# Attention feeding a two-GEMM block on one core: two pairs of TensorE steps joined into one step each, from batch 2 on

## The chip, the cores and the metric

The kernel runs on one core of a Trainium2 chip, in one launch. The metric is the device time in microseconds (us) of an execution, as the median over runs. The core has five engines that run side by side and wait for each other by semaphores: TensorE (PE, matrix multiplies), VectorE (DVE), ScalarE (ACT), GpSimd (POOL) and SyncE (SP, which only issues DMAs here). Each runs its own instructions in the order in which the program holds them.

## What is computed

The inputs q, k and v have 8 batches, 8 heads, 576 positions and 64 features each. The attention part adds two results: a pooled attention, over means of four positions, whose rows are repeated four times, and a local one, in which a position sees those less than 4 away. The sum, laid out as 4608 tokens by 512 features, goes through two matrix products with h * cos(h) between them.

```
factor = 4; Sd = S // factor; scale = 1.0 / np.sqrt(D)
q_d, k_d, v_d = (a.reshape(B, H, Sd, factor, D).mean(axis=3) for a in (q, k, v))
out_up = np.repeat(sm_attn(q_d, k_d, v_d), factor, axis=2)
mask = np.abs(pos[:, None] - pos[None, :]) < factor
scores = np.where(mask, scale * np.matmul(q, k.transpose(0, 1, 3, 2)), -1e9)
out_local = np.matmul(softmax(scores), v)
x = (out_up + out_local).transpose(0, 2, 1, 3).reshape(B * S, H * D)
h = x @ w_in                      # 512 -> 2048
return (h * np.cos(h)) @ w_out    # 2048 -> 512
```

## The kernel before

**The attention** works by pairs of heads: 8 batches of 4 pairs, called p0 to p3 here. For a pair, `u_qk` loads q and k and sums each over groups of four positions (`qkd`), `u_v` loads v in two layouts and sums it likewise (`vd`, `vl`), and three functions compute:
- `u_s`: on PE the local scores (`l_mm`, line 518: 48 small fp32 matmuls, 32 by 32 outputs, from q and k) and the pooled scores (`d_mm`, line 526: 4 matmuls of 72 by 144 from `qkd`), into two PSUM banks. Then, mostly on DVE, the mask (line 537), the maxima (542 and 550), their subtraction (389), the exponent on ACT, the sums (577), the reciprocal (581) and the scaling (583) of `sml` (local) and `smd` (pooled).
- `u_t`: the transposes of `smd` on PE (line 609, two steps, one a head) with copies into `ptd`, and of `sml` on DVE (600) into `ptl`.
- `u_pv`: on PE the pooled values (`d_mm`, line 626: 4 matmuls from `vd` and `ptd`) and the local values (`l_mm`, line 637: 48 matmuls from `vl` and `ptl`), the sum of both on DVE (645), and the split of the sum into a high and a low fp32r part, `xh` (660) and `xl` (389).

**The GEMMs** go over 12 token tiles of 384. `x` lies in a ring of four buffers, so the names x0 to x3 stand for tiles 0 to 3, then 4 to 7, and so on. For a tile and a chunk of 128 of the 2048 hidden features, `gemm1` (line 688) makes 12 matmuls of 128 by 384; ACT and DVE compute h * cos(h) from them (lines 697 to 706, `tr`, then `gh` and `gl`); `gemm2` (line 724) makes 9 matmuls of 128 by 512 with the results of two chunks earlier, in three steps. The first three tiles take four chunks in turn each, the rest run through all 16. The weights (`wi`, `wo`) come from 64-bit numbers; `w_split` takes them apart on ACT, DVE and POOL (lines 410 to 423) into a high and a low part, the low one by a subtraction (389).

**The order** is not written by hand. Each function hands its pieces of work to a planner, as `pl.op(engine, duration, function, reads, writes)`. The planner knows which piece depends on which, runs a list scheduling with estimated durations forth and back several times, keeps the best, and lets some pieces choose between two engines. The program is then emitted in the order of planned starts, so that one piece (a step) is never parted: all its instructions stand together on their engine, ahead of all later ones. The GEMM steps keep their order among themselves (`pe_order`); the attention steps fall in between. Where PE is planned to idle in the first 300 us, filler matmuls of an identity (line 841) are put in. `NEARLY = 2` separates the first two batches, which are computed before the GEMMs can run at full rate, from the others. The PSUM banks of the attention (`pa`) are three in rotation.

An example of a step as it is handed over:

```
pl.op("PE", 0.95, l_mm, r=[q, k], pw=banks, w=loc)
pl.op("PE", 0.65, d_mm, r=[qkd], pw=banks, w=poo)
```

Of the kernel before, what the change touches and what calls it, by code (L numbers as in the profile page):

```python
# [48 lines left out]
NEARLY = 2  # L49
# [241 lines left out]
def _dve(n):  # L291
    return n * 0.001042 + 0.065
# [7 lines left out]
def attn_ffn_kernel(ctx: ExitStack, tc: tile.TileContext, qT, kT, vdn, vl, w_in, w_out, out):  # L300
# [8 lines left out]
    pl = Plan()  # L309
# [92 lines left out]
    def w_split(k, c):  # L402
# [27 lines left out]
                k=([P, SP_], 1, 1, 0), ptd=([HD, 2, 2, SD], 1, 1, 0),  # L430
# [16 lines left out]
    def bank(b, kind):  # L447

        if b == 0:
            tags = ("pa.0", "po.0", "pa.1", "po.1") if kind == "s" else ("ph.0", "ph.1", "pa.2")  # L450
            return psum(tags[int(pl.turn("early" + str(kind == "s"), len(tags))[-1])])
        return psum(pl.turn("pa", 3))
# [47 lines left out]
    def u_s(b, pr):  # L500
        pl.name = "u_s"
        u = st[(b, pr)]
        q, k, qkd = u["q"], u["k"], u["qkd"]
        sml, smd = ub(b, pr, "sml"), ub(b, pr, "smd")
        banks = [bank(b, "s") for _ in range(2)]
        loc, poo = [pl.buf(None) for _ in banks], [pl.buf(None) for _ in banks]
# [5 lines left out]
        def l_mm():  # L512

            for n in range(2 * NSEG):
                for h in range(2):
                    for e in range(2):
                        hs, o, c = slice(64 * h, 64 * h + 64), (8 * (n // 4) + 4 * e + n % 4) * BQ, LQ + BS * (n % NSEG)
                        pe.matmul(banks[n // NSEG].get()[64 * h + BS * e:64 * h + BS * (e + 1), c:c + BS],  # L518
                                  q.get()[hs, o:o + BS], k.get()[hs, o:o + BS], start=True, stop=True)
        pl.op("PE", 0.95, l_mm, r=[q, k], pw=banks, w=loc)  # L520

        def d_mm():
            for i in range(2):
                for h in range(2):
                    hs = slice(64 * h, 64 * h + 64)
                    pe.matmul(banks[h].get()[:HD, i * SD:(i + 1) * SD], qkd.get()[hs, 0, i * HD:(i + 1) * HD], qkd.get()[hs, 1, :],  # L526
                              start=True, stop=True)
        pl.op("PE", 0.65, d_mm, r=[qkd], pw=banks, w=poo)


        mxl, su = sb("mxl", 2, [P, 2 * NSEG]), sb("su", 2, [P, 2 * NSEG + 4])
# [16 lines left out]
        for h in range(2):  # L548
# [3 lines left out]
            if not early:  # L552
                using(banks[h], pl.op("DVE", _dve(2 * SD), lambda h=h: dve.tensor_tensor(
                    out=smd.get()[:, h], in0=dq(h), in1=mxd.get()[:, h].unsqueeze(2).broadcast_to([HD, 2, SD]), op=ALU.subtract),
                    r=[poo[h], mx], pw=[smd]))
# [59 lines left out]
    def u_pv(b, pr):  # L615
        pl.name = "u_pv"
        u = st.pop((b, pr))
        ptl, ptd, vd, vt = (u[n] for n in ("ptl", "ptd", "vd", "vl"))
        xd, xs = ub(b, pr, "xd"), ub(b, pr, "xs")
        banks = [bank(b, "v") for _ in range(2)]  # L620
        poo, loc = pl.buf(None), [pl.buf(None) for _ in banks]

        def d_mm():
            for kh in range(2):
                for h in range(2):
                    pe.matmul(banks[0].get()[64 * h:64 * h + 64, 2 * SD:3 * SD], vd.get()[:, kh, 64 * h:64 * h + 64],  # L626
                              ptd.get()[:, h, kh, :], start=(kh == 0), stop=(kh == 1))
        pl.op("PE", 0.64, d_mm, r=[vd, ptd], pw=[banks[0]], w=[poo])

        def l_mm():  # L630
            for a in range(NSEG // 2):
                for i in range(4):
                    for e in range(2):
                        for h in range(2):
                            r = slice(64 * h + 32 * e, 64 * h + 32 * e + 32)
                            o = (4 * a + i) * BQ
                            pe.matmul(banks[e].get()[64 * h:64 * h + 64, o:o + BQ], vt.get()[r, a, i, :], ptl.get()[r, 4 * a + i, :BQ],  # L637
                                      start=True, stop=True)
        pl.op("PE", 1.52, l_mm, r=[vt, ptl], pw=banks, w=loc)

        evac(SD, xd.get, lambda: banks[0].get()[:, 2 * SD:3 * SD], banks[0], xd, scale=0.25)
        xd.w[-1].deps += poo.w
# [8 lines left out]
        while lo < S:  # L651
# [9 lines left out]
                  r=[xs], w=[done], pw=[x_b[tt]], alts=[("DVE", _dve(m / 2), lambda hi=hi, src=src: dve.tensor_copy(hi(), src()))])  # L661
            sub(m, lambda tt=tt, a=a, m=m: x_tile(tt)[1][:, pr, a:a + m], src, lambda hi=hi: hi().bitcast(F32),
                r=[xs, done], pw=[x_b[tt]])
# [94 lines left out]
    def unit(t, step, ahead, *a):  # L758
        for d, f in ((-ahead, u_qk), (0.01 - ahead, u_v), (0.0, u_s), (step, u_t), (2 * step, u_pv)):
            at(t + d, f, *a)  # L760

    for i in range(NPAIR):
        for t, f in ((-10.0 + 0.5 * i, u_qk), (-8.4 + 0.5 * i, u_v), (-7.5 + i, u_s), (-6.5 + i, u_t), (-5.5 + i, u_pv)):
            at(t, f, 0, i)
# [15 lines left out]
    for i in range(NPAIR):  # L780
        for t, f in ((-4.0 + 0.5 * i, u_qk), (-2.4 + 0.5 * i, u_v), (-0.9 + i, u_s), (-0.1 + i, u_t), (0.7 + i, u_pv)):
            at(t, f, 1, i)
# [96 lines left out]
```

## Time and profile before

| | |
|---|---|
| median of 3 runs | 1031.43 us (1028.47 to 1034.59) |
| the profiled execution | 1031.63 us, of it 1029.5 us from the first to the last instruction |
| mean granted PE clock | 0.983 |
| matmuls of an attention pair on PE | 96 each in local scores and local values (each fp32 matmul shows twice), 8 each in the other three steps |

The profile is of one execution. A page gives busy times, the span in 40 slices and the costliest groups; other views give the single instructions in order of time (start, duration, engine, line, output<-input, shape), in brackets the idle time of the engine before an instruction and the one that ended it, or busy times by stretches of the span. Durations of matmuls overlap, so that the distance between two starts tells what one costs.

### The profile page before, as it was taken

To read this page: it belongs to the slowest core of one execution; us is meant where nothing else is said; L and a number is where in the kernel's file an instruction comes from. 1 tells how busy PE (TensorE), PEld (TensorE's weight loads), DVE (VectorE), ACT (ScalarE), POOL (GpSimd) and SP (SyncE) were. 2 spreads that over 40 slices of the span, in tenths; PEclk is the share of its full clock that TensorE was granted. 3 is DMA by queue.
4 is the path that set the end of the run, shared out by engine and by line. 5 is a ranking of instruction groups with operands and counts; after the bars stand their busy time and mean duration, and the time that the engine had idled before them with its cause. 6 is when DMAs were issued, how large, how long until landed. Compare 5 with 4: busy or idle time off the path is not lost.

```text
span 1029.5 us, 25935 instructions
## 1 busy us (share of the span) xinstructions
PE 1003.0 (97%) x11068; PEld 864.9 (84%) x11068; DVE 676.9 (66%) x1353; ACT 610.6 (59%) x1176; POOL 228.8 (22%) x274
## 2 busy tenths in 40 slices
PE   7889999999999999999999999999999999999998
PEld 4557788889988888889898888888888888899997
DVE  6699889996478668564738856755646865543443
ACT  2546577786566666565646655655655765655554
POOL 5596424433135201010103300101002410000000
PEclk8988899999999999999999999999999999999999
DMA  9762751434245312100202401200101310000000
GB/s 265 237 221 85 242 183 46 61 59 62 32 106 144 76 50 75 59 25 28 76 6 76 133 28 38 96 25 28 55 27 43 120 51 1 32 1 1 31 1 31
DMA packets 36450, 76.11 MB, mean 74 GB/s; under 512 B 3440, under 2 KB 11632, under 8 KB 36336
## 3 DMA queue, kind: packets, MB, share of 16 engines
q1 hardware_dynamic: 32448, 67.38, 20.6%
q0 software_dynamic: 3888, 7.08, 5.0%
q8 instruction: 87, 1.43, 0.6%
q14 instruction: 27, 0.22, 0.1%
HBM read 57.93 MB, written 16.52 MB: 72 GB/s over the span
## 4 chain that ended last, share of the span: by engine, by line
PE 81%; DVE 10%; DMA 4%; ACT 2%; issue 2%; POOL 0%; SPq 0%; ACTq 0%; DVEq 0%; POOLq 0%
PE bank L688 35%; PE bank L724 35%; PE bank L637 3%; PE bank L518 3%; PE bank L526 2%; DMA q<-qT 2%; PE bank L609 2%; DMA wdi<-w_in 1%; PE bank L626 1%; DVE su L577 1%; DVE qkd L480 1%; DVE mxd L550 1%; PE bank L841 1%; DVE gl L389 1%; DVE tr L700 1%
## 5 line engine op out<-in xcount | busy, mean ns | idle before, releaser
L724 PE MATMUL bank<-wo,gh 128*128 128x512 f32 x1152 | 363.3, 396 | 0.0
L724 PEld LDWEIGHTS bank<-wo,gh 128*128 128x128 f32 x1152 | 210.0, 188 | 35.8 <-issue 2.3
L724 PE MATMUL bank<-wo,gl 128*128 128x512 f32 x576 | 228.0, 396 | 0.6 <-POOL su L535 0.6
L699 ACT ACTIVATE tr<-bank,bmagic 128x384 f32<-128x384 f32 x192 | 111.0, 579 | 134.0 <-PE bank L688 122.5
L703 DVE SCALAR_TENSOR_TENSOR tr<-tr,bank 128x384 f32<-128x384 f32 x192 | 105.3, 549 | 121.7 <-ACT tr L698 121.4
L700 DVE SCALAR_TENSOR_TENSOR tr<-tr,bank 128x384 f32<-128x384 f32 x192 | 105.5, 550 | 97.5 <-ACT tr L699 97.3
L697 ACT ACTIVATE tr<-tr 128x384 f32<-128x384 f32 x192 | 100.7, 524 | 84.4 <-DVE tr L700 83.7
L705 ACT ACTIVATE gh<-tr 128x384 fp32r<-128x384 f32 x177 | 92.5, 523 | 90.7 <-DVE tr L703 89.0
L389 DVE TENSOR_TENSOR gl<-tr,gh 128x384 fp32r<-128x384 f32 x160 | 97.3, 609 | 68.6 <-ACT gh L705 67.2
L724 PEld LDWEIGHTS bank<-wo,gl 128*128 128x128 f32 x576 | 108.0, 187 | 24.8 <-POOL su L535 1.0
L688 PE MATMUL bank<-x0h,wi 128*128 128x384 f32 x384 | 109.9, 347 | 0.7 <-DVE tr L703 0.7
L688 PE MATMUL bank<-x1h,wi 128*128 128x384 f32 x384 | 107.6, 341 | 0.0
L688 PE MATMUL bank<-x2h,wi 128*128 128x384 f32 x384 | 107.1, 339 | 0.0
L688 PE MATMUL bank<-x3h,wi 128*128 128x384 f32 x384 | 106.9, 339 | 0.0
L389 POOL TENSOR_TENSOR gl<-tr,gh 128x384 fp32r<-128x384 f32 x32 | 38.1, 1189 | 301.3 <-DVE gh L706 215.8
L698 ACT ACTIVATE tr<-tr 128x384 f32<-128x384 f32 x192 | 100.8, 525 | 6.1
L688 PEld LDWEIGHTS bank<-x0h,wi 128*128 128x128 f32 x384 | 72.1, 193 | 3.7 <-DVE tr L703 0.8
L688 PEld LDWEIGHTS bank<-x1h,wi 128*128 128x128 f32 x384 | 70.7, 189 | 2.9 <-issue 0.8
L688 PEld LDWEIGHTS bank<-x2h,wi 128*128 128x128 f32 x384 | 70.2, 188 | 2.8 <-DVE sml L537 0.6
L688 PEld LDWEIGHTS bank<-x3h,wi 128*128 128x128 f32 x384 | 70.2, 188 | 2.5 <-issue 0.6
L688 PE MATMUL bank<-x0l,wi 128*128 128x384 f32 x192 | 65.8, 342 | 0.0
L688 PE MATMUL bank<-x3l,wi 128*128 128x384 f32 x192 | 64.6, 336 | 0.5 <-POOL x3l L389 0.5
(192 smaller groups left out, 1473.0 us busy)
## 6 DMA issues: line engine op xcount, KB each, us to landing
vl<-vl SPq DMA_DIRECT2D x26, 384.0 KB
out<-ob SPq DMA_DIRECT2D x36, 256.0 KB
wdi<-w_in SPq DMA_DIRECT2D x16, 512.0 KB
wdo<-w_out SPq DMA_DIRECT2D x16, 512.0 KB
q<-qT SPq DMA_DIRECT2D x26, 292.0 KB
k<-kT SPq DMA_DIRECT2D x26, 292.0 KB
vd<-vdn SPq DMA_DIRECT2D x26, 288.0 KB
out<-ob POOLq DMA_DIRECT2D x27, 256.0 KB, 5.7
```

The lines of the kernel that those rows point to most:

```text
L389: f = lambda e: lambda: e.tensor_tensor(out=out(), in0=in0(), in1=in1(), op=ALU.subtract)
L518: pe.matmul(banks[n // NSEG].get()[64 * h + BS * e:64 * h + BS * (e + 1), c:c + BS], q.get()[hs, o:o + BS], k.get()[hs, o:o + BS], start=T ...
L526: pe.matmul(banks[h].get()[:HD, i * SD:(i + 1) * SD], qkd.get()[hs, 0, i * HD:(i + 1) * HD], qkd.get()[hs, 1, :], start=True, stop=True)
L637: pe.matmul(banks[e].get()[64 * h:64 * h + 64, o:o + BQ], vt.get()[r, a, i, :], ptl.get()[r, 4 * a + i, :BQ], start=True, stop=True)
L688: pe.matmul(ph.get()[:, :m], w[:, i, kc, :], x[:, kc, :], start=(n == 0), stop=(n == 3 * KC - 1))
L697: act.activation(tr.get(), tr.get(), AF.Sin, scale=PI)
L698: act.activation(tr.get(), tr.get(), AF.Square)
L699: pl.op("ACT", _act(m, True, 1), lambda: act.activation(tr.get(), h(), AF.Identity, bias=bmagic), r=[ph], w=[tr])
L700: pl.op("DVE", _dve(m), lambda: dve.scalar_tensor_tensor(out=tr.get(), in0=tr.get(), scalar=MAGIC, in1=h(), op0=ALU.subtract, op1=ALU.subt ...
L703: pl.op("DVE", _dve(m), lambda: dve.scalar_tensor_tensor(out=tr.get(), in0=tr.get(), scalar=0.5, in1=h(), op0=ALU.subtract, op1=ALU.mult), ...
L705: pl.op("ACT", _act(m, False), lambda: act.activation(gh.get(), tr.get(), AF.Copy), r=[tr], w=[gh], alts=[("DVE", _dve(m / 2), lambda: dve ...
L724: pe.matmul(o, (gh, gh, gl)[k].get()[:, sl], wo.get()[:, (0, 1, 0)[k]], start=(c == c0 and k == 0), stop=(c == c1 - 1 and k == 2))
```

## The change

For batches 2 to 7, `u_s` hands over its local and pooled scores as one step, local ones first, which reads q, k and `qkd`; `u_pv` hands over its pooled and local values as one step, pooled ones first, which reads `vd`, `ptd`, `vl` and `ptl`. The planned durations of the joined steps are 1.55 and 2.1, where the parts had 0.95 + 0.65 and 0.64 + 1.52. No matmul is added or removed, and batches 0 and 1 keep their separate steps. Since one plan is made for the whole program, the order and the choice of engines move in other places too.

```
-        pl.op("PE", 0.95, l_mm, r=[q, k], pw=banks, w=loc)
+        if b < NEARLY:
+            pl.op("PE", 0.95, l_mm, r=[q, k], pw=banks, w=loc)
...
-        pl.op("PE", 0.65, d_mm, r=[qkd], pw=banks, w=poo)
+        if b < NEARLY:
+            pl.op("PE", 0.65, d_mm, r=[qkd], pw=banks, w=poo)
+        else:
+            pl.op("PE", 1.55, lambda: (l_mm(), d_mm()), r=[q, k, qkd], pw=banks, w=loc + poo)
...
-        pl.op("PE", 0.64, d_mm, r=[vd, ptd], pw=[banks[0]], w=[poo])
+        if b < NEARLY:
+            pl.op("PE", 0.64, d_mm, r=[vd, ptd], pw=[banks[0]], w=[poo])
...
-        pl.op("PE", 1.52, l_mm, r=[vt, ptl], pw=banks, w=loc)
+        if b < NEARLY:
+            pl.op("PE", 1.52, l_mm, r=[vt, ptl], pw=banks, w=loc)
+        else:
+            pl.op("PE", 2.1, lambda: (d_mm(), l_mm()), r=[vd, ptd, vt, ptl], pw=banks, w=[poo] + loc)
```

After the change the lines named above stand 0 to 8 lines further down (526 is 527, 537 is 541, 609 is 613, 626 is 630, 637 is 642, 645 is 653, 688 is 696, 724 is 732, 841 is 849). Where the order is shown, the names stand for buffers with their numbers; in batches 0 and 1 a pair's tensors borrow the space of weights that come later, so that `wxi` and `wxo` are scores and values there too.

**In the full part**, on PE, about 640 us after the start, around chunks 14 and 15 of a tile. Before, one pair's scores and the values of the pair ahead of it stand in three places:

```order
L518 MATMUL bank<-k,q 32x32 x48
L526 MATMUL bank<-qkd 72x144 x4
L724 MATMUL bank<-wo_2977,gh 128x512 x2
L724 MATMUL bank<-wo_2977,gl 128x512
L626 MATMUL bank<-ptd,vd 64x144 x4
L688 MATMUL bank<-x2h,wi_3164 128x384
...
L637 MATMUL bank<-ptl,vl 64x24 x48
L724 MATMUL bank<-wo_3075,gh 128x512 x2
```

And at the same pairs with the change:

```order
L518 MATMUL bank<-k,q 32x32 x48
L527 MATMUL bank<-qkd 72x144 x4
L732 MATMUL bank<-wo_2848,gh 128x512 x2
L732 MATMUL bank<-wo_2848,gl 128x512
...
L630 MATMUL bank<-ptd,vd 64x144 x4
L642 MATMUL bank<-ptl,vl 64x24 x48
L696 MATMUL bank<-x2h,wi_3081 128x384
```

The pooled values moved behind the whole gemm2 and stand with the local ones; three islands of small matmuls became two. Counted over the program from the first gemm1 of tile 1 on, there are 80 such islands before and 74 now.

**In batch 1, between its pairs p2 and p3**, on PE. Before (`wxo_191` holds p2's pooled scores, `wxo_928` and `wxo_918` are p3's k and q, `wi_1378` is chunk 2 of w_in):

```order
L609 MATMUL bank<-ident,wxo_191 72x72 x4
L688 MATMUL bank<-x0h,wi_1378 128x384
L688 MATMUL bank<-x0l,wi_1378 128x384
...
L518 MATMUL bank<-wxo_928,wxo_918 32x32 x48
L526 MATMUL bank<-wxi_208 72x144 x4
L609 MATMUL bank<-ident,wxo_191 72x72 x4
```

With the change (chunk 2 is `wi_1358`, and p3's k and q are `wxo_925` and `wxo_910`; `wxi_270` with `wxo_315` are p1's local values, `wi_1477` is chunk 3):

```order
L696 MATMUL bank<-x0h,wi_1358 128x384
...
L642 MATMUL bank<-wxi_270,wxo_315 64x24 x48
L732 MATMUL bank<-wo_949,gh 128x512 x2
...
L613 MATMUL bank<-ident,wxo_191 72x72 x8
L518 MATMUL bank<-wxo_925,wxo_910 32x32 x48
L527 MATMUL bank<-wxi_208 72x144 x4
L630 MATMUL bank<-wxi_194 64x144 x4
L696 MATMUL bank<-x0h,wi_1477 128x384
```

The gemm1 of tile 0, chunk 2, which stood between p2's transposes and p3's scores, now stands ahead of p1's local values, and p3's scores follow p2's transposes directly.

**In batch 1, between p0 and p1**, on PE and DVE. Before, PE has p0's pooled and local values with nine fillers between them and no gemm1:

```order
L609 MATMUL bank<-ident,smd 72x72 x8
L518 MATMUL bank<-xxl 32x32 x48
L526 MATMUL bank<-wxi_126 72x144 x4
L626 MATMUL bank<-ptd,vd 64x144 x4
L841 MATMUL bank<-ident_b 128x512
...
L637 MATMUL bank<-ptl,vl 64x24 x48
```

With the change the gemm1 of tile 0, chunk 1 (`wi_1123`) stands there, behind four fillers:

```order
L613 MATMUL bank<-ident,smd 72x72 x8
L518 MATMUL bank<-xxl 32x32 x48
L527 MATMUL bank<-wxi_126 72x144 x4
L630 MATMUL bank<-ptd,vd 64x144 x4
...
L696 MATMUL bank<-x0h,wi_1123 128x384
L696 MATMUL bank<-x0l,wi_1123 128x384
...
L642 MATMUL bank<-ptl,vl 64x24 x48
```

The low half of that chunk's weight was made by POOL before; with the change DVE makes it, behind the subtraction of p1's maxima (`wxi_270` are p1's local scores):

```order
L541 TENSOR_TENSOR wxi_270<-bank,mask 128x192 x2
L554 TENSOR_REDUCE mxd<-bank 72x2
L546 TENSOR_REDUCE mxl<-wxi_270 128x12
L389 TENSOR_TENSOR wxi_270<-wxi_270,mxl 128x384
L389 TENSOR_TENSOR wi_1123<-xxh,wi_1123 128x512
L413 TENSOR_SCALAR xxh<-xxh 128x512
```

That gemm1, which stood behind p2's scores, now stands ahead of p0's local values, and so ahead of p1's transposes on PE. DVE has 178 instructions up to the last sum (line 645) of batch 1 before and 176 with the change; up to the second formula step (line 703) of the 25th gemm1 it has 348 and 334.

## The prediction, made before the result

> **What bounds the kernel now.** I read the head of the page first, then busy time by stretches, then who made TensorE (PE) wait after 150 us.
>
> ```profile
> span 1029.5 us, 25935 instructions
> PE 1003.0 (97%) x11068; PEld 864.9 (84%) x11068; DVE 676.9 (66%) x1353; ACT 610.6 (59%) x1176; POOL 228.8 (22%) x274
> ...
> PEclk8988899999999999999999999999999999999999
> ```
> ```profile
> 53.00:115.00 62.00, 53.64 (x989) 37.48 (x985) 56.68 (x110) 32.82 (x90) 44.43 (x47) 0.82 0.53 174
> ...
> 114.15:1025.50 911.35, 907.64 (x9059) 803.37 (x9054) 586.09 (x1172) 557.00 (x1018) 155.59 (x173) 1.00 0.21 57
> ```
> ```profile
> PE bank L609 <- DVE smd L583: 1.4, 5, 0.4
> PE bank L688 <- DVE tr L703: 0.7, 1, 0.7
> PE bank L688 <- POOL x3l L389: 0.5, 1, 0.5
> ```
>
> The columns of the stretches are length, then busy PE, weight loads, DVE, ACT, POOL, then the clock and the DMA. From 114.15 us to the last matmul PE is busy 907.64 of 911.35 us at clock 1.00; after 150 us it waits 2.6 us in all (1.4 + 0.7 + 0.5). In that part the time is the sum of PE's work, so only less PE work, or a new wait, can move the end. Ahead of it stands a part where PE is not the bound: from 53 to 115 us DVE is busy 56.68 of 62 us while PE runs at clock 0.82, partly on filler matmuls. This is the attention of batch 1's four pairs (p0 to p3), which gemm1 of token tile 1 has to have. So there are two places: what an attention step costs PE in the full part, and when the full part begins.
>
> **Term 1: fewer interruptions of the GEMM stream.** No matmul is removed. What can fall away is the cost of going from the full-array GEMM matmuls to the small ones and back. Here the timeline of PE around one pair's scores and another's values (start, duration, instruction):
>
> ```profile
> 639.76 0.40 PE L724 MATMUL bank<-wo,gl 128*128 128x512 f32 x1
> 640.09 1.02 PE L518 MATMUL bank<-k,q 64*32 64x32 f32 x96
> 641.04 0.71 PE L526 MATMUL bank<-qkd 64*72 64x144 f32 x8
> 641.68 0.73 PE L724 MATMUL bank<-wo,gh 128*128 128x512 f32 x2
> 642.25 0.40 PE L724 MATMUL bank<-wo,gl 128*128 128x512 f32 x1
> ...
> 645.24 0.34 PE L688 MATMUL bank<-x2h,wi 128*128 128x384 f32 x1
> 645.50 1.59 PE L637 MATMUL bank<-ptl,vl 32*64 32x24 f32 x96
> 647.03 0.73 PE L724 MATMUL bank<-wo,gh 128*128 128x512 f32 x2
> 647.59 0.39 PE L724 MATMUL bank<-wo,gl 128*128 128x512 f32 x1
> 647.82 0.62 PE L724 MATMUL bank<-wo,gh 128*128 128x512 f32 x2
> 648.29 0.40 PE L724 MATMUL bank<-wo,gl 128*128 128x512 f32 x1
> ...
> 654.41 0.71 PE L626 MATMUL bank<-ptd,vd 72*64 72x144 f32 x8
> 655.06 1.59 PE L637 MATMUL bank<-ptl,vl 32*64 32x24 f32 x96
> 656.58 0.44 PE L688 MATMUL bank<-x3h,wi 128*128 128x384 f32 x1
> ```
>
> Undisturbed, a gemm2 matmul is followed by the next after 0.23 us (647.59 to 647.82) and two take 0.47 (647.82 to 648.29). Into an island of small matmuls it is 0.33 us (639.76 to 640.09), 0.10 more; out of it the first two take 0.57 (641.68 to 642.25), 0.10 more. The island at 645.50 shows the same 0.10 at its end (0.56 from 647.03). An island thus costs 0.20 us beside its work. Inside one a change of kind shows nothing of the sort: pooled values take 0.65 us with local values behind them (654.41 to 655.06), pooled scores 0.64 with a gemm behind them. By the order of PE, 80 islands follow the first gemm1 of tile 1 before, and 74 now: the split ones (values alone 12, pooled scores alone 2) are gone, but pooled and local scores stood together already in nearly all pairs, and pooled values often hung on a scores island, so that pulling them to the local values frees no island. 6 x 0.20 = 1.2 us less. Bounds: 6 x 0.10 = 0.6, if only one edge goes, and 14 x 0.20 = 2.8, if every split island counted.
>
> The Trainium skill, "TensorEngine Tiling (Array Packing)", Key Properties, says that a change of tiling mode drains TensorE. By it a merged step still pays at its inner change, so about half would be saved, 0.6 us. The 0.65 against 0.64 us above shows no inner drain, so the trace's 1.2 stands.
>
> **Term 2: the part before PE is full.** The steps of batches 0 and 1 are unchanged, but their order is not. The chain there runs: a pair's scores on PE, mask, maximum, exponent, sum and scaling on DVE and ACT, its transposes on PE, then the next pair's scores.
>
> ```profile
> 64.28 0.62 DVE L537 TENSOR_TENSOR wxi<-bank,mask 128x192 f32<-128x192 f32 x2 [1.56 <-PE bank L526]
> ...
> 66.01 0.77 DVE L389 TENSOR_TENSOR wxi<-wxi,mxl 128x384 f32<-128x384 f32 x1
> ```
> ```profile
> 69.29 1.59 PE L637 MATMUL bank<-ptl,vl 32*64 32x24 f32 x96
> 70.81 1.90 PE L841 MATMUL bank<-ident_b 128*128 128x512 bf16 x8
> 74.46 0.72 PE L609 MATMUL bank<-ident,wxi 72*72 72x72 f32 x7 [1.75 <-DVE wxi L583]
> ...
> 89.73 0.67 PE L609 MATMUL bank<-ident,wxo 72*72 72x72 f32 x4 [2.10 <-DVE wxo L583]
> 90.14 0.67 PE L688 MATMUL bank<-x0h,wi 128*128 128x384 f32 x1
> ...
> 93.78 1.02 PE L518 MATMUL bank<-wxo,wxo 64*32 64x32 f32 x96
> 94.74 0.71 PE L526 MATMUL bank<-wxi 64*72 64x144 f32 x8
> ...
> 105.42 0.69 PE L609 MATMUL bank<-ident,wxi 72*72 72x72 f32 x8
> ...
> 115.32 0.69 PE L688 MATMUL bank<-x1h,wi 128*128 128x384 f32 x1
> ```
> ```profile
> 95.48 0.62 DVE L537 TENSOR_TENSOR wxi<-bank,mask 128x192 f32<-128x192 f32 x2 [2.14 <-PE bank L526]
> ```
>
> At p2 to p3, gemm1 of tile 0, chunk 2 stands between p2's first transposes (89.73) and p3's scores (93.78), and DVE, the bound of this part, idles 2.14 us for those scores. Now that gemm1 runs ahead of p2's transposes, and p3's scores follow them at once. They then start near 90.5 (89.73 and both sets of transposes, 0.7 us as at 105.42), 3.3 us earlier. What stands against it: two gemm1 results (L700) now lie on DVE ahead of p2's mask, about 1 us; and at p0 to p1 the gemm1 of chunk 1 comes ahead of p0's local values. That one needs chunk 1's low half, which DVE now makes right behind p1's subtraction: 66.01 + 0.69 + 0.68 = 67.4 us, later if DVE's added work there (a value sum and two weight steps) overfills its 1.56 us of slack. I book 0.6 us for that. Up to the last sum (L645) of batch 1 DVE runs 176 instructions instead of 178, at 56.68/110 = 0.52 us each 1.0 us less. Together -3.3 + 1.0 + 0.6 - 1.0 = -2.7; I take -2.0, since only 2.14 us of the gap is seen as idle time of the bound. Bounds: DVE idles 62.00 - 56.68 = 5.3 us in this part, so -6.3 with the 1.0, and no gain at all, or the loss of the first slow rival.
>
> Does the gain survive? After the start of the full part DVE paces the weight splits. Up to the second formula step (L703) of the 25th gemm1 its order holds 334 instructions instead of 348, since batch 2's second pair comes later. At 0.52 us each that is a lead of several us for DVE, so a PE that starts 2 us earlier is not caught by it.
>
> **Term 3: new waits.** A merged step waits for q, k and their pooled forms together, or for both kinds of weights and values, with the GEMMs queued behind it on PE. In nearly all pairs the two parts already followed one another, so the wait was there (L609 for DVE is the only recurring one, 1.4 us in five). Pooled values moved back to the local ones wait for less. Ahead of gemm1 of tile 3 the order now has two fillers, 2 x 0.23 = 0.46 us of PE; before, that gemm1 waited 0.5 us there for POOL's x3l. I take +0.4 us in all; bounds -2.6 (all waits gone) and +3 (as much again).
>
> **Sum.** The profiled execution took 1031.63 us: 1031.63 - 1.2 - 2.0 + 0.4 = 1028.8. The median of the runs, 1031.43, lies 0.2 lower: 1028.6 us. A measurement of this kernel tells a change from none at about 0.5%, 5.2 us, so this is "no change" with a lean to faster.
>
> **Rivals.**
> - The early gain doesn't come: DVE, in order, takes up the freed gap with what it now does sooner, and only terms 1 and 3 stay, 1031.4 - 1.2 + 0.4 = 1030.6. For it: DVE's instruction count falls by 2 only. Against: 2.14 us of plain waiting for PE. Chance 0.26.
> - The early part gains all that DVE idles there: -6.3 - 1.2 gives 1024. For it: the fillers between the first gemm1 and that of tile 1 fall from 53 to 48. Against: waits shift rather than vanish. Chance 0.15; faster by over 0.5%.
> - Slower: the gemm1 of chunk 1 blocks PE. p0's local values, p1's transposes and p2's scores are queued behind it. To keep p1's transposes at 74.46, it must start by 74.46 - 1.7 (7 fillers) - 1.5 (values) - 3.5 (a gemm1 at the clock of this part) = 67.8. Before, POOL made that half at
>
> ```profile
> 78.03 1.27 POOL L389 TENSOR_TENSOR wi<-xxh,wi 128x512 fp32r<-128x512 f32 x1
> ```
>   and such a landing, 79.3, would set the chain back 11.5 us: 1028.6 + 11.5 = 1040. It turns the sign from a landing near 71 on, and passes 0.5% from 76. Against: that subtraction is now DVE's and stands early in its order. Chance 0.08.
> - Slower by the clock: in this part a gemm1 takes 3.45 us where the full clock gives 2.10.
>
> ```profile
> 90.40 3.45 PE bank L688 x12
> ...
> 120.53 2.10 PE bank L688 x12
> ```
>   If the new order leaves PE emptier, three gemm1 and all small steps run slow for longer, some 3 x 1.35 = 4 us plus a third of the four pairs' small steps (about 4 us each: 5 us), 1028.6 + 9 = 1038. The Trainium skill, "TensorE: Matmul & The Clock Gate", Why this matters for your kernels, warns of idle gaps over about 3 us between bursts; here no wait above is longer than 2.4 us, and the clock is at 0.82 all the same. Chance 0.06.
>
> **How the numbers follow.** My forecast, 1028.6, holds from 1026 to 1030 with 0.45. The faster rival lies at 1024, the flat one at 1030.6, the slow ones at 1038 to 1040. The range 1023.5 to 1035.5 takes in the first three and part of the waits' bound (+3), and leaves out about 2 in 10. Over 0.5% faster (below 1026.3): the faster rival and the forecast's lower edge, 0.22. Over 0.5% slower (above 1036.6): 0.13. The rest, 0.65, is the same.
>
> **What would show it.** Right: the first gemm1 of tile 1 starts near 113 instead of 115.3; DVE's wait for p3's scores is gone; from there PE stays over 99% busy; 74 islands, each with 0.1 us at either edge. Wrong: p1's transposes well after 76 us; that gemm1 after 116; PE waits after 150 us well over 2.6 us; or a new order of DVE that makes PE wait for the results of h * cos(h).

## The result, and the profile after

The changed kernel takes 1025.61 us in the median of 7 runs (1022.94 to 1029.27), the kernel before beside it 1031.43 (1028.47 to 1036.81): a ratio of 0.9944, 95% interval [0.9923, 0.9966]. Measured once more later, it took 1027.72 (12 runs) against 1032.24, 0.9955 [0.9932, 0.9978]. Forecast were 1028.6 us, in a range of 1023.5 to 1035.5. The profiled execution took 1025.61 us.

The head of its page, the two stretches that were shown of before (length, then busy PE, weight loads, DVE, ACT, POOL, clock, DMA share, GB/s), and all waits of PE after 150 us:

```profile
span 1023.9 us, 25921 instructions
PE 999.4 (98%) x11062; PEld 865.3 (85%) x11062; DVE 676.5 (66%) x1356; ACT 611.9 (60%) x1176; POOL 224.5 (22%) x269
...
PEclk9988999999999999999999999999999999999999
```
```profile
53.00:111.50 58.50, 50.57 (x977) 35.81 (x977) 52.49 (x103) 33.75 (x93) 41.38 (x42) 0.85 0.56 184
110.70:1020.00 909.30, 906.11 (x9066) 804.92 (x9066) 587.68 (x1178) 557.99 (x1017) 148.71 (x170) 1.00 0.21 57
```
```profile
PE bank L613 <- DVE smd L587: 2.6, 1, 2.6
```

The picture is the one of before: PE full from about 111 us on, DVE the busiest in the stretch ahead of it. The full part, from the first gemm1 of tile 1 to the last matmul, went from 909.42 to 907.34 us, and it began at 111.80 instead of 115.32. So of 6.0 us between the two profiles 3.5 lie ahead of the full part, 2.1 in it, and 0.4 around the span.

The joined steps on PE in the full part (start, duration, instruction), and the milestones of the early part in the timeline:

```profile
634.13 1.02 PE L518 MATMUL bank<-k,q 64*32 64x32 f32 x96
635.08 0.71 PE L527 MATMUL bank<-qkd 64*72 64x144 f32 x8
...
638.01 0.71 PE L630 MATMUL bank<-ptd,vd 72*64 72x144 f32 x8
638.65 1.59 PE L642 MATMUL bank<-ptl,vl 32*64 32x24 f32 x96
```
```profile
61.69 1.30 PE L613 MATMUL bank<-ident,smd 72*72 72x72 f32 x8 [2.77 <-ACT smd L593]
...
67.86 0.88 PE L696 MATMUL bank<-x0h,wi 128*128 128x384 f32 x1
...
74.75 0.78 PE L613 MATMUL bank<-ident,wxi 72*72 72x72 f32 x8 [0.26 <-DVE wxi L587]
...
90.28 1.18 PE L613 MATMUL bank<-ident,wxo 72*72 72x72 f32 x8
91.38 1.51 PE L518 MATMUL bank<-wxo,wxo 64*32 64x32 f32 x96
...
102.79 0.72 PE L613 MATMUL bank<-ident,wxi 72*72 72x72 f32 x8 [0.56 <-DVE wxi L587]
...
111.80 0.44 PE L696 MATMUL bank<-x1h,wi 128*128 128x384 f32 x1
```

The inner change costs nothing again (0.64 us from the pooled to the local values, 638.01 to 638.65). The gemm1 of chunk 1 started at 67.86 and p1's transposes at 74.75, against 74.46 before, so it blocked nothing. p3's transposes came 12.5 us after p2's (90.28 to 102.79), against 15.7 before (89.73 to 105.42).

One wait is left in the full part, ahead of the first gemm1 of tile 3. It comes from SP: its queue issued a pair's loads late (it had waited 5.4 us for DVE's value sums), q was there 7.4 us after its issue, DVE, in order, waited for it, and the sums and the scaling of the pair that PE needed stood behind. SP, DVE and PE there:

```profile
305.90 0.32 SPq L487 DMA_DIRECT2D vd<-vdn  x1
306.31 0.35 SPq L466 DMA_DIRECT2D q<-qT  x1
```
```profile
313.71 0.75 DVE L480 TENSOR_REDUCE qkd<-q 128x144 f32<-128x576 f32 x1 [3.29 <-DMA q<-qT]
314.45 0.75 DVE L480 TENSOR_REDUCE qkd<-k 128x144 f32<-128x576 f32 x1
...
317.62 0.74 DVE L587 TENSOR_TENSOR smd<-smd,su 72x576 f32<-72x576 f32 x1
```
```profile
318.50 0.66 PE L613 MATMUL bank<-ident,smd 72*72 72x72 f32 x8 [2.60 <-DVE smd L587]
...
319.48 0.84 PE L696 MATMUL bank<-x3h,wi 128*128 128x384 f32 x2
```

Behind the wait two gemm1 matmuls take 0.84 us; at full clock they take 0.51 (below).

### The profile page after: what moved, and what is told of

It is laid out like the page before. It is cut to its first block, busy times and chain, and to the rows that moved or that the text cites. A ratio compares the mean times of both kernels' runs of the same rounds, so it can differ in the third digit from the quotient of the medians.

```text
span 1023.9 us, 25921 instructions
## 1 busy us (share of the span) xinstructions
PE 999.4 (98%) x11062; PEld 865.3 (85%) x11062; DVE 676.5 (66%) x1356; ACT 611.9 (60%) x1176; POOL 224.5 (22%) x269
## 4 chain that ended last, share of the span: by engine, by line
PE 93%; DVE 4%; DMA 1%; issue 1%; ACT 0%; POOL 0%; SPq 0%; ACTq 0%
PE bank L696 39%; PE bank L732 39%; PE bank L642 5%; PE bank L518 3%; PE bank L527 2%; PE bank L630 2%; PE bank L613 2%; PE bank L849 1%; DMA q<-qT 1%; DMA wxo<-kT 0%; DVE xxh L417 0%; DVE wxi L587 0%; DVE mxd L554 0%; DVE su L581 0%; DVE xxh L411 0%
## 5 line engine op out<-in xcount | busy, mean ns | idle before, releaser
L708 DVE SCALAR_TENSOR_TENSOR tr<-tr,bank 128x384 f32<-128x384 f32 x192 | 105.2, 548 | 91.3 <-ACT tr L707 90.5
L389 DVE TENSOR_TENSOR gl<-tr,gh 128x384 fp32r<-128x384 f32 x161 | 93.1, 579 | 69.7 <-ACT gh L713 68.2
L713 ACT ACTIVATE gh<-tr 128x384 fp32r<-128x384 f32 x163 | 85.3, 524 | 81.0 <-DVE tr L711 80.0
L389 POOL TENSOR_TENSOR gl<-tr,gh 128x384 fp32r<-128x384 f32 x31 | 34.6, 1116 | 297.3 <-DVE gh L714 247.7
```

What stands on the lines that cost most here:

```text
L389: f = lambda e: lambda: e.tensor_tensor(out=out(), in0=in0(), in1=in1(), op=ALU.subtract)
L708: pl.op("DVE", _dve(m), lambda: dve.scalar_tensor_tensor(out=tr.get(), in0=tr.get(), scalar=MAGIC, in1=h(), op0=ALU.subtract, op1=ALU.subt ...
L713: pl.op("ACT", _act(m, False), lambda: act.activation(gh.get(), tr.get(), AF.Copy), r=[tr], w=[gh], alts=[("DVE", _dve(m / 2), lambda: dve ...
```

## The experiments

The first question was whether the early or the full part had gained. To answer it, both plans, the separate and the joined one, were built in one kernel and their orders put together or edited by hand. `seq_s` is the emission order of the kernel before, `seq_j` that of the changed one; lines of the edited kernels stand 0 to 1 further down than in the changed kernel.

**The two orders crossed.** One kernel goes by the old order up to the first gemm1 of tile 1 and by the new one from there, the other the reverse.

```
-    seq = seq_j
+    seq = then(seq_s, seq_j, 1, 0)      # early_old_late_new; the other: then(seq_j, seq_s, 1, 0)
```

> The order of the kernel before up to the first gemm1 of tile 1, and from there the order of the changed kernel, with the joined steps (the two fillers of the later part left out). Theory A (two places: the early part begins the full part 3.5 us sooner, and the full part saves 6 islands of 0.2 us and some waits): the first gemm1 of tile 1 stays near 115.3 us, 74 islands, and the time is 1031.4 - 1.4 - 0.7 = about 1029. Theory B (the whole gain comes from the joined steps in the full part): about 1025.6.

> The order of the changed kernel up to the first gemm1 of tile 1, and from there the order of the kernel before, with separate steps (80 islands). Theory A: the first gemm1 of tile 1 starts near 111.8 us and runs at the full clock, so 1031.4 - 3.5 - 0.9 = about 1027. Theory B: 1031.4.

Old order first, new one behind: 1027.60 us against 1031.37, ratio 0.9965 [0.9945, 0.9986]. New order first, old one behind: 1030.89, 0.9994 [0.9973, 1.0016]. Theory A had 1029 and 1027 us, theory B 1025.6 and 1031.4: the first kernel lies between the two, the second at B. The full part took 907.43 us with the new order (here without its two fillers) and 909.90 with the old one, much as in the unedited kernels. So the gain of the full part belongs to its order and is shown; the early order's isn't visible in these times. The profiles say why a gain there is hard to see: with the same early order the first gemm1 of tile 1 started at 111.80 in one execution and at 117.02 in this one.

**p3's scores first.** In the kernel before, the gemm1 of tile 0, chunk 2 moves behind p3's scores and nothing else moves on PE: the step on which term 2 of the prediction rests.

```
+    x = seq.pop(cut_at(seq, 0, 2))
+    seq.insert(at(seq, "u_s", (1, 3), "PE", True) + 1, x)
...
```

> The kernel before with one thing moved: the gemm1 of tile 0, chunk 2, stands behind p3's scores in batch 1 instead of ahead of them. Theory A1 (that gemm1 in the chain of pairs is what the early part loses): DVE's wait of 2.1 us for p3's scores goes, the first gemm1 of tile 1 starts at 113 to 113.5 us, and the time is about 1029.4. Theory A2 (DVE's own work bounds the early part, and the gain there came from other moves of the plan): it starts at 115 us still, 1031.4.

1031.84 us, ratio 1.0003 [0.9984, 1.0022], and the first gemm1 of tile 1 at 116.17 us. Its PE, DVE and POOL (p3's scores, p3's transposes; the work of DVE and POOL between):

```profile
89.51 0.62 PE L519 MATMUL bank<-wxo,wxo 64*32 64x32 f32 x48
...
105.33 0.72 PE L614 MATMUL bank<-ident,wxi 72*72 72x72 f32 x8 [1.18 <-DVE wxi L588]
```
```profile
90.93 2.65 DVE L390 TENSOR_TENSOR gl<-tr,gh 128x384 fp32r<-128x384 f32 x1
...
95.82 0.61 DVE L542 TENSOR_TENSOR wxi<-bank,mask 128x192 f32<-128x192 f32 x2
```
```profile
90.36 1.27 POOL L390 TENSOR_TENSOR wi<-xxh,wi 128x512 fp32r<-128x512 f32 x1
```

The first row of DVE and POOL's work at that time in the kernel before:

```profile
90.84 0.51 DVE L389 TENSOR_TENSOR gl<-tr,gh 128x384 fp32r<-128x384 f32 x1
```
```profile
91.23 0.60 POOL L389 TENSOR_TENSOR x1l<-wxi,x1h 128x192 fp32r<-128x192 f32 x1 [2.26 <-ACT x1h L660]
```

And DVE from p2's to p3's transposes, here and in the kernel before (length, busy DVE, clock, DMA share, GB/s):

```profile
89.20:105.30 16.10, 15.52 (x30) 1.00 0.86 300
```
```profile
89.73:105.42 15.69, 13.55 (x31) 0.89 0.58 178
```

p3's scores start 4.3 us earlier than before (89.51 against 93.78), but its mask starts at 95.82 instead of 95.48, and p3's transposes come at 105.33 instead of 105.42. DVE's rows ahead of the mask are the same as before, a sum, a transpose, a low half, a formula step and two weight steps, and no wait for the scores is left between them: the low half alone took 2.65 us where it had taken 0.51, as much as the 2.14 us for which DVE had waited. No more than these 2.1 of the 4.3 us could be had, then, and none were: the gap was filled not with more work but with a longer row. POOL ran beside the whole of it (from 90.36 us on, without a gap), where in the kernel before it had idled for 2.26 us up to 91.23. That fits the 14 profiles: none of the 769 DVE rows that took over 1.5 times the shortest of the same operation, tiles and shape in their profile ran without POOL at work beside it, while 72% of the other rows did. No run moves POOL's rows alone, so for this row that cause is likely and not shown. The time, the same as before within 0.2%, doesn't speak for a gain either.

**p3's scores later.** The reverse, in the changed kernel: nine fillers ahead of p3's scores.

```
+    seq[g] = (o, e, (9, next(b for _, b in sep.banks if o in b.acc)), k)   # g: the local scores of p3, batch 1
```

> The changed kernel with nine fillers, about 3.5 us of PE at the clock of that part, put ahead of the scores of the last pair of batch 1 (p3). Theory of the prediction (PE's way from p2's transposes to p3's scores is on the path that sets the first gemm1 of tile 1): the time from p2's to p3's transposes grows by about 3 us, from 12.0 to 12.5 to over 15, and the time from the first gemm1 of all to the first one of tile 1 from 58 to 60.5 to over 61. Rival (DVE's own work bounds that stretch, as the run with p3's scores put first suggested): DVE has other work to do meanwhile, and both intervals grow by less than 1 us.

DVE's mask of p3 in the changed kernel, with the scaling of its pooled scores, and the mask here:

```profile
94.08 0.62 DVE L541 TENSOR_TENSOR wxi<-bank,mask 128x192 f32<-128x192 f32 x2 [1.91 <-PE bank L527]
...
101.27 1.38 DVE L587 TENSOR_TENSOR wxi<-wxi,su 72x576 f32<-72x576 f32 x1
```
```profile
97.09 0.62 DVE L542 TENSOR_TENSOR wxi<-bank,mask 128x192 f32<-128x192 f32 x2 [4.23 <-PE bank L528]
```

The one run took 1025.55 us, no more than the changed kernel: its full part took 903.95 us, with a wait of only 0.63 us ahead of tile 3, so only the intervals tell. DVE waits 2.3 us longer, p3's transposes come 15.0 us after p2's instead of 12.5, and the first gemm1 of tile 1 comes 63.3 us after the first gemm1 of all, against 59.2 in the changed kernel's first profile. So in the new order PE's way is on the path again. In the changed kernel's first profile, from p2's transposes to p3's mask it takes 3.8 us (90.28 to 94.08) where it took 5.75 (89.73 to 95.48), and from the mask to the start of the scaling DVE takes 7.2 us (94.08 to 101.27, 17 rows of that timeline) where it took 8.6 (95.48 to 104.11, 20 rows). So the 3.2 us between p2's and p3's transposes lie in the way to the mask, some 1.9, and in the fewer DVE rows behind it, some 1.4. PE's part alone gave nothing in the old order; DVE's alone wasn't tried.

**The pooled scores split off.** The changed kernel with the pooled scores held back behind the next GEMM step, in 22 pairs.

```
+            x = seq.pop(d)                 # the pooled scores of a pair
...
+            if seq[g][0].name in ("gemm1", "gemm2"):   # g: the next PE step
+                seq.insert(g + 1, x)
```

> The changed kernel with the pooled scores of 22 pairs held back behind the GEMM step that follows the local ones: 96 islands instead of 74, everything else in the same order. If an island costs 0.20 us beside its work: 1025.6 + 4.4 = 1030.0, and PE's edges grow by 4.4 us in the profile. If half of that is paid at the inner change of a joined step anyway: 1025.6 + 2.2 = 1027.8. Where the later scores make DVE late, more.

1034.20 us, ratio 1.0022 [0.9999, 1.0045]. The full part takes 913.34 us, 6.0 more than 907.34, with 96 islands instead of 74. Its timeline at one pair:

```profile
640.69 1.02 PE L519 MATMUL bank<-k,q 64*32 64x32 f32 x96
641.64 0.73 PE L733 MATMUL bank<-wo,gh 128*128 128x512 f32 x2
642.21 0.40 PE L733 MATMUL bank<-wo,gl 128*128 128x512 f32 x1
642.53 0.71 PE L528 MATMUL bank<-qkd 64*72 64x144 f32 x8
```

Out of the new island the first two gemm2 matmuls take 0.57 us (641.64 to 642.21) instead of 0.47, and into it the last takes 0.32 (642.21 to 642.53) instead of 0.23. Summed over the full part the edges (what the steps into and out of islands take more than undisturbed ones) cost 16.99 us against 12.13: 4.86 us for 22 islands, 0.22 each, close to the 0.20 that term 1 took from two rows. Over all 74 islands the mean is less, 0.16. The other 1.1 us of the 6.0 isn't assigned.

**Joining without a new plan.** The kernel before, with the scores joined at the place of the later of the two, and the values likewise, in batches 2 to 7; then the same with the values alone.

```
...                                      # for every pair (b, i) of batches 2 to 7
+    for f in ("u_s", "u_pv"):            # values_only: "u_pv" alone
+        x = seq.pop(at(seq, f, (b, i), "PE"))
+        seq.insert(at(seq, f, (b, i), "PE"), x)
```

> The order of the kernel before, with one edit in batches 2 to 7: each pair's pooled scores follow its local scores at once, and its pooled values move down to its local values. No step is placed anew otherwise. Counted in this order, the full part has 76 islands of small matmuls between GEMM steps, against 80 before and 74 in the changed kernel. Theory (merging islands is what the full part gained): 4 islands fewer at 0.20 us, so about 908.6 us against 909.4 to 909.9, and of the 2.1 to 2.5 us that the full part gained some 0.8 belong to the merging and the rest to the new placing of the steps. Rival (the gain of the full part is all in the new placing): 909.4 to 909.9 as before. Second rival (a merged step waits for the later of its two inputs): new waits of PE of over 0.3 us at transposes or values, and a full part over 910.

1041.02 us, ratio 1.0091 [1.0060, 1.0122]: slower than before, as the second rival had it. The full part takes 918.44 us with 76 islands; the edges fell to 12.77 us as forecast (13.55 before), but PE's waits over 0.1 us rose from 3.25 to 9.98. PE, POOL and SP at the longest one:

```profile
170.43 1.02 PE L519 MATMUL bank<-k,q 64*32 64x32 f32 x96
...
180.47 0.80 PE L733 MATMUL bank<-wo,gl 128*128 128x512 f32 x1 [5.60 <-POOL gl L390]
181.06 1.05 PE L733 MATMUL bank<-wo,gh 128*128 128x512 f32 x2
```
```profile
171.53 0.34 SPq L467 DMA_DIRECT2D q<-qT  x1
```
```profile
174.83 0.44 POOL L474 TENSOR_TENSOR qkd<-q 128x144 f32<-128x144 f32 x1 [8.44 <-DMA q<-qT]
```

The local scores, moved down to the pooled ones, read q and k until 171.4 us. Only then can SP load the next pair's q into that space (171.53; before, 152.26). POOL, in order, waits 8.44 us for it, `gl` stands behind, and gemm2 waits 5.60 us for `gl`, and runs its next matmuls in pairs of 1.05 us instead of 0.62.

> As join_only, but only the values are joined (in batches 2 to 7 each pair's pooled values move down to its local ones); the scores stay where they were. 77 islands. join_only took 918.44 us for the full part, 9.98 of them waits, and its longest, 5.60 us at 180.47, was POOL, in order, behind the DMA of q, issued at 171.53, right after the moved local scores had read q and k (171.4); before, it was issued at 152.26. Theory (a joined score step holds the buffers of q and k until the pooled forms' turn comes, and the next pair's loads with them): without the joined scores that DMA is issued near 152 to 153 again, the 5.60 us wait is gone, the waits of the full part are back at 3 to 4 us, and it takes 908.5 to 909.5. Rival (the later pooled values hold something too, the buffers of vd and the transposed weights): the full part stays over 911.

1029.81 us in one run. q is issued at 149.35 us and the 5.60 us wait is gone; the waits are 4.93 us and the full part 909.76 us. So it was the joined scores that held the buffers. By this one profile joining by itself, even of the values alone, gains nothing here: 909.76 against 909.42 to 909.90.

**The two reductions of q and k moved.** The changed kernel, with the two DVE rows that waited for q (313.71) behind the scaling that PE waited for.

```
+    late = [x for x in seq[g - 60:end] if x[0].name == "u_qk" and x[1] == "DVE"]
+    late = late[-2:]
...
+    seq = [x for x in seq if x not in late]
...
+    seq[end + 1:end + 1] = late          # end: behind the scaling of the pair ahead of gemm1 [tile 3, chunk 0]
```

> The changed kernel's order with one edit: the two DVE reductions of q (L480 of the changed kernel), which waited 3.29 us for the DMA of q at 313.71 us with the sums and the scaling of the pair in front of gemm1 [tile 3, chunk 0] queued behind them, stand behind that scaling. Theory (the order of the instructions alone makes the length of the full part, and its last long wait is this one): the wait of the transposes, 2.60 us at 318.50, goes, and so does the half-clock stretch of the gemm1 behind it (about 1.3 us); the full part takes about 903.5 instead of 907.34 us, and the time is about 1022. Rival (PE only waits a step later, for x3l of POOL or for the q formula, since the same work still has to be done before the same gemm1): a wait of 1.5 to 2.5 us turns up within 10 us of that place, and the full part stays within 1 us of 907.3.

1023.67 us, ratio 0.9927 [0.9902, 0.9951]. The same place on PE:

```profile
314.53 0.67 PE L614 MATMUL bank<-ident,smd 72*72 72x72 f32 x8
...
315.43 0.51 PE L697 MATMUL bank<-x3h,wi 128*128 128x384 f32 x2
```

No wait, full clock (0.51 us a pair), and none over 0.1 us anywhere in the full part, which takes 904.31 us, 3.0 less than in the changed kernel's first profile. The rival's wait a step later didn't come. What the edit is worth changes from execution to execution, though: with the same order and without the edit the wait was 2.60, 1.59, 1.29 and 0.63 us and the full part took 907.34, 905.91, 905.15 and 903.95 us (the kernel itself, after_again, warm1, delay), and the interval of the ratio overlaps that of the unedited kernel.

**One filler instead of two, and both edits.**

```
-           fgap=0.4, f0=0.8, fend=300.0, warm=2)
+           fgap=0.4, f0=0.8, fend=300.0, warm=1)
```

> The changed kernel with one filler instead of two ahead of each early step of TensorE (some 96 fillers ahead of the full part instead of 116). Theory (the fillers are on the chain in batch 0, where almost every PE step between 21 and 47 us follows two of them): 20 fewer at 0.23 to 0.27 us, so the first gemm1 comes up to 5 us earlier, at 48 to 51 instead of 52.6 us, and the time is 1021 to 1023. Rival (the fillers hold up the granted clock, as a page of the Trainium skill, TensorE: Matmul & The Clock Gate, would have it of filler work in idle gaps): with fewer of them the steps of batch 0 and of the first gemm1 run at the lower clock, two fillers' worth of time is lost again at each, and the first gemm1 comes at 53 to 57 us, with a time of 1026 to 1031.

> Both edits that gained: the two reductions of q and k behind the scaling (qkd_late), and one filler instead of two (warm1). Theory (independent places, so the gains add): qkd_late stood at 0.9927 of the kernel before and warm1 at 0.9913, the changed kernel at 0.9944, so about 0.990, 1021 us, with the full part near 904 and no wait of PE over 0.3 us in it. Rival (warm1 gained by chance, and one filler leaves the early clock as it finds it): 1023 to 1024, as qkd_late alone.

One filler: 1024.44 us, 0.9913 [0.9878, 0.9947]; with the reductions moved too: 1022.96, 0.9909 [0.9873, 0.9944]. The first gemm1 came at 54.7 and 53.4 us, no earlier than with two fillers, so the mechanism that I gave for a gain isn't there, and the interval of the one filler overlaps that of the unedited kernel. In its profile late_and_one has a full part without a wait, 903.03 us. It has the lowest median here, 9.3 us faster than the kernel before (1032.24) and 4.8 faster than the changed one (1027.72) beside it; the intervals of the two ratios, [0.9873, 0.9944] and [0.9932, 0.9978], just overlap.

**p0's scaling ahead of p1's value sums.** qkd_late, with one DVE step of batch 1 moved.

```
+    x = [x for x in seq[:end] if x[0].name == "u_v" and x[1] == "DVE"][-1]   # end: the last DVE step of p0's scores
...
+    seq.remove(x)
...
+    seq.insert(end + 1, x)
```

> qkd_late with one more edit on DVE in batch 1: the two value sums of p1 (L494 and L495 of the changed kernel), which stand ahead of p0's reciprocal (59.59 to 60.89 us there), move behind p0's scaling. In the four runs with the changed kernel's order in the first two batches p0's transposes came 9.1 to 10.8 us after the first gemm1, against 7.8 to 8.0 with the order before, and the first gemm1 of tile 1 59.2 to 60.9 us after the first gemm1. Theory (these two rows hold up the chain at p0): p0's transposes come 1.3 us sooner, 7.8 to 9.5 us after the first gemm1, and the first gemm1 of tile 1 57.9 to 59.6 us after it; the full part stays at 904.3. Rival (DVE has the same work in all, and its own work bounds the way to the first gemm1 of tile 1): p0's transposes come sooner, but that interval stays at 59.2 to 60.9. The time alone, 1022 to 1024 by either, can't tell them apart; the intervals do.

1025.47 us, 0.9930 [0.9912, 0.9948]. p0's transposes waited 3.40 us for their scaling instead of 4.56, but the first gemm1 of tile 1 still came 61.2 us after the first gemm1. Of these, 2.76 us are a wait that the edit has nothing to do with ("issue", last section); without it they are 58.4, against 57.3 to 58.9 in the order without the edit. So the rival holds: the 1.2 us that p0's transposes gained don't reach the first gemm1 of tile 1.

**The changed kernel again.**

> The changed kernel once more, unedited, beside the kernel before and the edited ones on the same chip. By both theories 1024 to 1027 us, the full part 906 to 907.5, with the wait of the transposes near 318 to 322 between 0.6 and 2.6 us, by how long the DMA of q takes (5.7 to 7.4 us from issue to use in the runs so far). What is open is the start: the first gemm1 of tile 1 came at 111.8 here, 117.0 and 114.4 in two other runs with the same order ahead of it. If the early part had gained what the two first profiles showed (3.5 us), it comes near 112 again; if that was the granted clock of one execution, anywhere from 111 to 117.

1027.72 us, as at the top. In its profile the full part begins at 115.89 us and takes 905.91. Its wait ahead of tile 3 is 1.59 us, and the gemm1 behind it runs at full clock. The start near 112 us, as in the first profile, didn't come again in this one.

## Why the prediction was right or wrong, point by point

**The sum** was right in sign and within 3 us of both measurements, though the change measured (5.8 and 4.5 us) is larger than the one forecast (2.8). Its parts were not all right, and that the sum came so near is in part luck: one term had its size for another reason than the one given, another had the wrong sign. All of it is the gain of one new plan; whether a new plan without the joined steps would have gained as much wasn't tried. The early orders of both kernels stand in four profiles each (the edits left the order up to there alone). All times in us; "issue wait" is the stop just ahead of the full part that the last section explains, and the fourth row takes it out:

| | order before | order after |
|---|---|---|
| first gemm1 of all | 53.3, 54.4, 53.3, 54.8 | 52.6, 56.5, 55.0, 49.9 |
| first gemm1 of tile 1 | 115.3, 115.9, 113.2, 116.2 | 111.8, 117.0, 115.9, 109.2 |
| between the two | 62.0, 61.5, 59.9, 61.4 | 59.2, 60.5, 60.9, 59.3 |
| without the issue wait | 61.0, 60.8, 59.3, 61.1 | 58.9, 58.9, 58.9, 57.3 |
| p2's to p3's transposes | 15.7, 14.3, 14.3, 15.9 | 12.5, 12.0, 12.5, 12.0 |
| first gemm1 to p0's transposes | 8.0, 7.8, 7.8, 7.8 | 9.1, 10.8, 10.2, 10.8 |

(Before: the kernel itself, early_old_late_new, values_only, join_only. After: the kernel itself, early_new_late_old, after_again, qkd_late.)

**Term 1, islands: right.** 74 islands instead of 80. Their edges cost 13.55, 13.41 and 13.36 us in three profiles of the old order, and 12.13, 12.21 and 11.77 in three of the new: 1.4 us less, forecast 1.2. The rule of the Trainium skill, "TensorEngine Tiling (Array Packing)", Key Properties, by which the inner change would pay too, gave 0.6; the measurements stand with the rows.

**Term 2, the early part: size right, mechanism not.** Without the issue wait the way from the first gemm1 to that of tile 1 fell from 60.6 to 58.5 us in the mean, 2.1; I had taken 2.0. (Further stops of the same sort, of 0.2 to 1.0 us at p3's local values in three profiles of the new order and of 0.35 us in join_only, are left in; without them it is 2.5.) But the step by which p3's scores "then start near 90.5", 3.3 us earlier, with the chain behind them, failed: scores_first did just that and gained nothing, since DVE, in order, took up the gap, as the first rival had it, if with a longer row and not with more work. The sign that I had named, that DVE's wait for p3's scores is gone, came only in part: the wait is 1.91 and 1.64 us in the two profiles of the changed kernel and under 0.1 in the two others of the new order, against 2.14, 0.74, 0.80 and 2.31 in the old one. The 2.8 us that p2 to p3 gained in the mean came with fewer DVE rows as well. And I had left out a loss: p0's transposes came 2.4 us later behind the first gemm1, since p1's value sums now stand ahead of p0's reciprocal on DVE and the scaling moved to ACT (the wait of 2.77 us at 61.69). DVE in the changed kernel, and the reciprocal before:

```profile
59.59 0.68 DVE L494 TENSOR_TENSOR wxi<-wxi 72x512 f32<-72x512 f32 x1
60.30 0.66 DVE L495 TENSOR_TENSOR wxo<-wxi 72x256 f32<-72x256 f32 x1
60.89 0.24 DVE L585 RECIPROCAL su<-su 128x16 f32<-128x16 f32 x1
```
```profile
59.94 0.23 DVE L581 RECIPROCAL su<-su 128x16 f32<-128x16 f32 x1
```

I had only looked for the loss where a GEMM step moved. As vsum_late shows, that loss can't be had back by moving those sums alone.

How much of term 2 reaches the end is open: the start of the first gemm1 itself varies by 6.6 us from execution to execution of one order, and the crossed kernel measured 0.6 us with an interval of some 2 us to either side.

**Term 3, waits: wrong in sign.** Forecast were +0.4 us with the two new fillers; PE's waits over 0.1 us in the full part fell from 3.25, 3.51 and 3.95 us in three profiles of the old order to 2.60, 2.04 and 1.59 in three of the new, 1.5 less, or 1.2 with the fillers, which cost 0.5 us in the two of these three that have them. This is most of what the full part gained beyond the forecast: it took 909.42, 909.90 and 909.52 us in the old order and 907.34, 907.43 and 905.91 in the new, 2.7 less, where terms 1 and 3 had 0.8. Edges (-1.4), waits (-1.5) and fillers (+0.3 in the mean) make 2.6 of it. But two of the three new profiles also pay some 1.5 us for a slow gemm1 behind their wait (last section), 1.0 in the mean, so that about 1 us of the gain is unassigned. The step that failed is "in nearly all pairs the two parts already followed one another, so the wait was there": it counted places and not times. All short waits went, those for `smd`, for POOL's `su` and `x3l` and for `tr`, and one other came, for a DMA. I had read which waits a merged step would have, but not when a merged step frees its buffers and when SP, DVE and POOL take up the loads behind it. join_only shows that this is the real price of joining: without a new plan around it, it costs 9 us.

**The slow rivals** didn't happen: the gemm1 of chunk 1 started at 67.86 us, where 67.4 was worked out for its low half, and the clock of the early part was 0.85 against 0.82. The faster one, all of DVE's idle time, didn't either: in the first profile DVE still idles 58.50 - 52.49 = 6.0 us there.

## What to carry to other kernels

A join of two steps is paid for where buffers are freed: ask which loads wait for the earlier half and what stands in order behind those loads; here the join cost 9 us when it was put into the old order, while the new plan that came with it gained about 5 in all. A wait of an engine for its partner is no gain in hand: here one of 2.14 us went, and a longer row of the same engine took its place. And where a start varies by several us between executions of one order, take one profile's start for no gain: compare intervals inside the profile, over several runs.

## What the runs showed of the hardware that I had not expected

**The clock falls after a wait of about 2 us.** The 12 matmuls of the first gemm1 of tile 3 took 3.82 us behind waits of 2.60 and 2.04 us and 3.67 behind 2.12, but 2.26 to 2.29 behind 1.59, 1.29, 0.63 and none, all at the same place of the new order. So at this place a wait of 2 us costs some 1.5 us on top of itself. The granted clock in those two stretches, of the changed kernel and of qkd_late (length, busy PE, clock):

```profile
318.90:322.40 3.50, 3.50 (x17) 0.56 0.00 0
```
```profile
315.00:317.30 2.30, 2.30 (x20) 1.00 0.31 107
```

The Trainium skill, "TensorE: Matmul & The Clock Gate", Why this matters for your kernels, sets that limit at gaps of over about 3 us; at this one place it lay between 1.59 and 2.04.

**A step can stop without a semaphore, until its instructions are loaded.** Just ahead of the full part, batch 2's first local scores are parted after 86 of 96 matmuls by a wait that no engine releases, called "issue". In the changed kernel, and in vsum_late:

```profile
110.81 0.41 PE L518 MATMUL bank<-k,q 64*32 64x32 f32 x10 [0.32 <-issue]
```
```profile
115.22 0.42 PE L519 MATMUL bank<-k,q 64*32 64x32 f32 x10 [2.76 <-issue]
```

It took 0.3 to 2.8 us in one and the same order of PE, and in some runs (late_and_one, delay) it wasn't there; the gemm1 behind it took 2.19 us in the first case and 4.00 in the last. The traces show what ends such stops. There are 76 of over 0.1 us in the 14 profiles, most of them in the first 53 us, and each time PE goes on 1.2 to 1.7 us after the end of a 16 KB transfer on the DMA queue that the profile names "instruction" (a transfer ended at 109.53 us for the stop that ended at 110.81, and at 113.66 for 115.22); times picked blindly between 60 and 125 us lie in that distance from a transfer in 6% of the cases. The page of the changed kernel has of this queue (packets, MB, share of 16 engines):

```profile
q8 instruction: 87, 1.43, 0.6%
```

That is one transfer for every 256 of PE's 22124 matmuls and weight loads, and the stops stand at fixed places of PE's order, such as after 1868 and after 1996 matmuls in the new one, which is 128 matmuls and 128 weight loads. So what PE waits for there are its own instructions. No run changed how they are loaded.

The stops and the clock are why one order starts its full part anywhere from 109.2 to 117.0 us. In the seven profiles with the new order and two fillers, the stops ahead of the first gemm1 sum to 2.9 us where it starts first (49.9) and to 5.6 to 7.9 in the others. Without them it would start at 45.4 us where the mean clock between 20 and 53 us was 0.95, at 46.4 to 47.1 where it was 0.86 to 0.90, and at 48.2, 48.5 and 50.9 where it was 0.80, 0.76 and 0.66.
